# Seam into the third matrix product: conversion in shorter bursts, column pairs of 384/448/448, weights loaded step by step, more output buffers

## The chip, the cores and the metric

One core of one Trainium2 chip runs the whole program. The metric is the time of one execution on the device in microseconds (us), as the median of several runs. Smaller is better.

## The reference, cut to what matters

Inputs are `q`, `k`, `v` of shape (8, 8, 576, 64) in float32, and four weight matrices that arrive as 64-bit floats; the output is float32.

```python
q_s = softmax(q, axis=-1);  k_s = softmax(k, axis=2)          # with +1e-9 under the sums
attn = einsum('bhsd,bhde->bhse', q_s, einsum('bhsd,bhse->bhde', k_s, v))
x = attn.transpose(0, 2, 1, 3).reshape(4608, 512)
h = x @ moe_w_in                       # 512 -> 2048
g = h * (1 / (1 + exp(-1.702 * h)))
x = g @ moe_w_out                      # 2048 -> 512
h = x @ moe2_w_in                      # 512 -> 2048
g = where(h >= 1, h, where(h <= -1, 0, (h + 1) ** 2 / 4))
out = g @ moe2_w_out                   # 2048 -> 512
```

So there is one attention without a score matrix and then four matrix products over 4608 tokens.

## The kernel before, in words

Every matrix product is done on pairs (high, low) of float32r numbers: each product of a weight and an operand is three matrix multiplications (high·high, high·low, low·high). All but the first part of the first product use a seven-product scheme (Strassen-Winograd): weights and operands are split into quadrants, seven sums of quadrants are multiplied, and sums of the results give the output.

The stretches of the program, in order:

1. **Attention with the first product for four blocks.** Tokens come in nine blocks of 512. Blocks 0, 1, 2 and 4 (`CL`) are multiplied directly in 64 steps of 12 matrix multiplications (`gemm1`, L1038 to L1040). The attention of all nine blocks is laid between these steps; the table `AT` gives the step at which each block's attention starts. Results of the five other blocks go to DRAM (`xs_dram`).
2. **The pair stretch**: the first product for the remaining five blocks, 2560 tokens, with the seven-product scheme (`gemm_b`, L1358). It has 3 pairs × 4 groups × 7 products = 84 steps of 12 matrix multiplications. `PAIRS` says how many columns a step has. Behind each step, `post_b` lets ScalarE copy a bank of PSUM or VectorE add one (L209, "a sum" below); ScalarE then applies the activation (L1394) and SyncE stores the result to `g0_dram` (L1397). The stored tiles take turns in the buffers of the list `EB`.
3. **Pass 2**: the second product (`gemm2`, L1509), 5 token blocks × 7 products × 4 = 140 steps of 12. Its operands are tiles of `g0_dram`, loaded by `load_g` (L1488), split by ScalarE (high, L1190) and VectorE (low, L209) into the buffers of the list `RING`. Its weights are seven tiles of 2 MB (`load_weight`, L344), one per product.
4. **Two more passes** of 140 steps each, for the third and the fourth product (L605, L487).

The class `Weights` converts the 64-bit weights of the second, third and fourth product, each in 8 pieces while an earlier stretch runs: per piece two raw loads (L240), the conversion (L178 on ScalarE, L184 and L191 on VectorE), seven sums of quadrants and their high and low parts (L282, L209, L292), and seven stores to `wp_dram` (L304). The pieces of the second product's weights ("out1") are made during the pair stretch; pass 2 loads them from there.

A planner (`Plan.order`) puts all of this in one order per engine: each entry has an engine, an estimated duration, a rank (measured in steps), what it reads and writes, and a bonus in rank (`haste`). Engines then execute their own queue strictly in that order, SyncE too: a transfer that must wait for a buffer holds back all transfers behind it in SyncE's queue. `LAST` is 64, the rank of the first step of the pair stretch, and `NEXT` is 148, the rank of the first step of pass 2.

The lines by which the second product's weights and first operands are asked for:

```python
w_new.everything([LAST + 2 + 8 * i for i in range(8)], later)
...
for x, (tag_i, p) in zip((-13, -12, -6, -4.9, -3.9, -2.9, 0), enumerate(ORDER)):
    load_w2(w_out1, "out1", p, tag_i, NEXT + x)
for i in range(4):
    load_g(0, "11", i, NEXT - 11 + i / 4)
    load_g(0, "22", i, NEXT - (5.9, 5.8, 4.8, 4.7)[i])
    load_g(0, "12", i, NEXT - (3.8, 3.7, 2.8, 2.7)[i])
```

Of the kernel before, what the change touches and what calls it, by code (L numbers as in the profile page):

```python
# [98 lines left out]
def kernel(  # L99
# [112 lines left out]
    class Weights:  # L212
        W = 128

        def __init__(self, w, at):
            self.w, self.at, self.n, self.kept = w, at, 0, None
            self.src = {"out1": w1_out, "in2": w2_in, "out2": w2_out}[w]
            self.raw_n, self.f_n = ((w, "r", 0), (w, "r", 1)), tuple((w, "f", i) for i in range(4))
            self.h_n = ((w, "h", 0), (w, "h", 1)) + self.raw_n
# [1112 lines left out]
    def load_x(jj, qd):  # L1332
        j, c = cut(jj, int(qd[1]) - 1)
        t = x_t[jj, qd] = slot(QB[qd])[:, :, :PAIRS[jj][0]]
        nc.sync.dma_start(out=t, in_=xs_dram[j, int(qd[0]) - 1][:, :, c])
# [353 lines left out]
```

## Time and profile before

| what | value |
|---|---|
| runs | 1587.96 us median of 3 (1583.99 to 1588.44) |
| the profiled execution | 1590.3 us; its span, first to last instruction, 1588.3 us |
| TensorE busy | 1493.2 us, 94% of the span |
| VectorE busy | 1126.9 us, 71% |
| ScalarE busy | 894.5 us, 56% |
| TensorE's granted clock, mean | 0.977 of full speed |
| pair stretch | starts at 267.3 us |
| pass 2 | first multiplication at 494.5 us, last one ends at 888.8 us |

How to read it: the span is what the trace shows; the execution's own time has 2.0 us more around it. TensorE is the busiest engine, so time is lost where it stands idle or runs at a lower clock. In the views below PE is TensorE's matrix multiplications, PEld its weight loads, DVE is VectorE, ACT is ScalarE, SP is SyncE and SPq its queue of transfers.

### The profile page before, as it was taken

To read this page: it belongs to the slowest core of one execution; us is meant where nothing else is said; L and a number is where in the kernel's file an instruction comes from. 1 tells how busy PE (TensorE), PEld (TensorE's weight loads), DVE (VectorE), ACT (ScalarE), POOL (GpSimd) and SP (SyncE) were. 2 spreads that over 40 slices of the span, in tenths; PEclk is the share of its full clock that TensorE was granted. 3 is DMA by queue.
4 is the path that set the end of the run, shared out by engine and by line. 5 is a ranking of instruction groups with operands and counts; after the bars stand their busy time and mean duration, and the time that the engine had idled before them with its cause. 6 is when DMAs were issued, how large, how long until landed. Compare 5 with 4: busy or idle time off the path is not lost. (4 is left out here: it accounts for less than half of the span.)

```text
span 1588.3 us, 21360 instructions
## 1 busy us (share of the span) xinstructions
PE 1493.2 (94%) x7920; PEld 1285.5 (81%) x7920; DVE 1126.9 (71%) x1410; ACT 894.5 (56%) x1132; POOL 6.2 (0%) x27
## 2 busy tenths in 40 slices
PE   5999999999944799999999999999999999999998
PEld 3878777888843578778899888888999888888998
DVE  7999953564522679697976657585775788795885
ACT  5877774565621354545444468787786544443443
POOL 0000000000000000000000000000000000000000
PEclk9999999999986899999999999999999999999999
DMA  9978753676787375847477755564658981534441
GB/s 286 275 210 243 217 191 152 237 265 252 247 328 314 108 269 154 274 148 257 146 226 274 280 202 218 213 218 183 239 194 294 420 292 48 157 134 133 134 120 40
DMA packets 257656, 341.16 MB, mean 215 GB/s; under 512 B 93840, under 2 KB 214672, under 8 KB 254864
## 3 DMA queue, kind: packets, MB, share of 16 engines
q1 hardware_dynamic: 256752, 339.70, 62.8%
q8 instruction: 62, 1.02, 0.3%
q14 instruction: 42, 0.34, 0.1%
q10 hardware_dynamic: 800, 0.10, 0.0%
HBM read 196.08 MB, written 143.65 MB: 214 GB/s over the span
## 5 line engine op out<-in xcount | busy, mean ns | idle before, releaser
L209 DVE TENSOR_TENSOR s<-s,s 128x1024 fp32r<-128x1024 f32 (+6 forms) x692 | 608.4, 919 | 237.9 <-ACT s L1190 68.6
L1509 PE MATMUL z<-s,w 128*128 128x512 f32 (+1 forms) x1440 | 311.5, 376 | 64.2 <-ACT s L1190 50.0
L1509 PEld LDWEIGHTS z<-s,w 128*128 128x128 f32 x1440 | 267.0, 192 | 105.7 <-ACT s L1190 50.9
L1190 ACT ACTIVATE s<-s 128x1024 fp32r<-128x1024 f32 (+2 forms) x168 | 161.3, 968 | 152.3 <-PE z L1509 92.1
L455 ACT ACTIVATE s<-s 128x1024 fp32r<-128x1024 f32 (+1 forms) x140 | 136.2, 976 | 174.2 <-PE zx L487 62.1
L487 PE MATMUL z<-s,w 128*128 128x512 f32 (+1 forms) x1008 | 210.6, 368 | 0.3 <-DVE s L209 0.3
L605 PE MATMUL z<-s,w 128*128 128x512 f32 (+1 forms) x960 | 208.6, 369 | 2.4 <-ACT s L1190 2.4
L487 PEld LDWEIGHTS z<-s,w 128*128 128x128 f32 x1008 | 183.7, 188 | 25.0 <-DVE s L209 0.7
L605 PEld LDWEIGHTS z<-s,w 128*128 128x128 f32 x960 | 176.0, 189 | 25.6 <-ACT s L1190 2.8
L605 PE MATMUL zx<-s,w 128*128 128x512 f32 (+1 forms) x720 | 157.7, 367 | 0.4 <-issue 0.4
L605 PEld LDWEIGHTS zx<-s,w 128*128 128x128 f32 x720 | 131.3, 188 | 17.6 <-issue 0.8
L487 PE MATMUL zx<-s,w 128*128 128x512 f32 (+1 forms) x648 | 135.1, 367 | 0.0
L487 PEld LDWEIGHTS zx<-s,w 128*128 128x128 f32 x648 | 117.9, 188 | 15.0
L1358 PE MATMUL z<-s,w 128*128 128x512 f32 (+1 forms) x576 | 116.1, 354 | 0.7 <-ACT s L1394 0.7
L1358 PEld LDWEIGHTS z<-s,w 128*128 128x128 f32 x576 | 96.4, 190 | 16.2 <-ACT s L1394 0.9
L1038 PE MATMUL hps<-s,w 128*128 128x512 f32 x256 | 104.4, 408 | 0.0
L1040 PE MATMUL hps<-s,w 128*128 128x512 f32 x256 | 100.3, 392 | 0.0
L1039 PE MATMUL hps<-s,w 128*128 128x512 f32 x256 | 100.1, 391 | 0.0
L1358 PE MATMUL zx<-s,w 128*128 128x512 f32 (+1 forms) x432 | 88.3, 354 | 2.4 <-ACT s L1190 1.6
L1358 PEld LDWEIGHTS zx<-s,w 128*128 128x128 f32 x432 | 72.1, 189 | 14.1 <-ACT s L1190 1.8
L209 DVE TENSOR_TENSOR s<-s,z 128x1024 f32<-128x1024 f32 (+2 forms) x58 | 63.7, 1099 | 25.1 <-PE z L1358 8.6
L655 ACT ACTIVATE s<-s 128x1024 f32<-128x1024 f32 (+1 forms) x80 | 77.6, 969 | 1.0
(102 smaller groups left out, 1445.5 us busy)
## 6 DMA issues: line engine op xcount, KB each, us to landing
g<-s SPq DMA_DIRECT2D x112, 512.0 KB, 3.1
s<-g SPq DMA_DIRECT2D x96, 512.0 KB, 5.6
wp_out<-s SPq DMA_DIRECT2D x112, 256.0 KB, 2.9
w<-wp_out SPq DMA_DIRECT2D x14, 2048.0 KB, 15.1
s<-g SPq DMA_DIRECT2D x48, 384.0 KB, 4.2
s<-in_moe_w_out_dram SPq DMA_DIRECT2D x32, 512.0 KB, 4.3
wp_in<-s SPq DMA_DIRECT2D x56, 256.0 KB, 4.2
w<-wp_in SPq DMA_DIRECT2D x7, 2048.0 KB, 10.2
```

The source lines that it names most:

```text
L209: return nc.vector.tensor_tensor(out=o, in0=x, in1=y, op=op)
L455: first_of[s] = nc.scalar.activation(out=hi, in_=src, func=ACTF.Copy)
L487: nc.tensor.matmul(out=z[:, m, :n], lhsT=a, rhs=b[:, c, :], start=(at is not None and i == 0 and c == 0 and x == 0), stop=(i == 3 and c == ...
L605: nc.tensor.matmul(out=z[:, m, :n], lhsT=a, rhs=b[:, c, :], start=(p in OPENS and c == 0 and x == 0), stop=(c == 1 and x == 2), skip_group ...
L655: nc.scalar.activation(out=got["t"], in_=got["t"], func=ACTF.Square)
L1038: nc.tensor.matmul(out=hps, lhsT=wh, rhs=ah, start=(kk == 0), stop=False)
L1039: nc.tensor.matmul(out=hps, lhsT=wh, rhs=al, start=False, stop=False)
L1040: nc.tensor.matmul(out=hps, lhsT=wl, rhs=ah, start=False, stop=(kk == KD - 1))
L1190: nc.scalar.activation(out=o, in_=x, func=ACTF.Copy)
L1358: nc.tensor.matmul(out=zb[jj, g, a][:, m, :n], lhsT=w[:, f], rhs=y[:, c, :], start=(p in OPENS and c == 0 and x == 0), stop=(c == 1 and x ...
L1509: nc.tensor.matmul(out=zs2[j, a][:, m, :n], lhsT=y, rhs=b[:, c, :], start=(first and c == 0 and x == 0), stop=(i == 3 and c == 1 and x == ...
```

## The change

Six things change together.

- **Pieces of a conversion** (all three weight matrices): two raw buffers in place of one, so that both raw loads of a piece are asked for at once; the entries of one piece lie within 4.5 steps in place of 7.3. For "out1" the pieces start 5.3 steps apart from rank 58.9 in place of 8 steps apart from rank 66, and have a bonus of 1 in rank in place of a malus of 3.
- **Columns of the pairs**: 384, 448, 448 in place of 512, 512, 256. The pairs now cut across the blocks, so that a tile is loaded or stored in up to two transfers.
- **Attention** of the last seven blocks starts 6.0 steps apart (from 8.6) in place of 6.55 (from 7.5).
- **Weights of pass 2**: two of the seven are asked for before pass 2 starts (at NEXT − 16.9 and − 13.9), the other five at NEXT + 0.5, 4, 8, 12 and 16. Tiles of `g0_dram` for the first block are asked for earlier.
- **Output buffers** of the pair stretch: 4 in the first pair, 5 in the second, 8 in the third, in place of 4 throughout.
- **Operand buffers of pass 2**: the first two steps take theirs from `RING` too, whose order is changed.

```diff
-            self.raw_n, self.f_n = ((w, "r", 0), (w, "r", 1)), tuple((w, "f", i) for i in range(4))
-            self.h_n = ((w, "h", 0), (w, "h", 1)) + self.raw_n
+            self.f_n, self.h_n = (tuple((w, x, i) for i in range(4)) for x in "fh")
+            self.raw_n = self.h_n[:2], self.h_n[2:]
...
-                self.kept = a, h(b) + (c[:, :512], c[:, 512:768]), h(d) + h(a)
+                self.kept = (a, d), h(b) + (c[:, :512], c[:, 512:768]), h(a) + h(d)
...
-            w, n, x = self.w, self.W, self.n % 4
+            w, n, x = self.w, self.W, (0, 1, 2, 3, 0, 1, 2)[self.n % 7]
...
-                    self.load(si, h, later(s0 + 2 * h))
-                    self.convert(h, later(s0 + 2 * h + 1.5))
+                    self.load(si, h, later(s0 + 0.1 * h))
+                    self.convert(h, later(s0 + 1.3 + 0.5 * h))
                 for part in range(4):
-                    self.sums(si, part, later(s0 + 4.5 + 0.8 * part))
+                    self.sums(si, part, later(s0 + 2.3 + 0.6 * part))
...
-    AT.update({j: (7.5 + 6.55 * (j - 2), 10.8 + 6.55 * (j - 2)) for j in range(2, NB)})
+    AT.update({j: (8.6 + 6.0 * (j - 2), 8.6 + 3.3 + 6.0 * (j - 2)) for j in range(2, NB)})
...
-    PAIRS = ((TB, (3, 5)), (TB, (6, 7)), (TB // 2, (8, 8)))
+    REST = [j for j in range(NB) if j not in CL]
+    PAIRS = ((384, 0), (448, 768), (448, 1664))
...
-    EB = (24, 25, 26, 18)
+    E1, E2 = (24, 25, 26, 18), (19, 20, 21, 22)
+    EB = E1 * 4 + (24, 25, 26, 18, 19) * 4
+    EB = EB[:32] + (E1 + E2) * 2
...
     def cut(jj, t):
-        n, blocks = PAIRS[jj]
-        return blocks[t], slice(t * n, t * n + n) if blocks[0] == blocks[1] else slice(0, n)
+        n, t0 = PAIRS[jj]
+        return [(off, m, REST[x], slice(c, c + m)) for off, m, x, c in segs(t0 + t * n, n, TB)]
...
+            def kept():
+                for off, m, j, c in parts:
+                    nc.sync.dma_start(out=g0_dram[j][a * 4 + g][:, :, c], in_=got[0][:, :, off:off + m])
...
-    hand(LAST + 0.9, sl(*WB), w_new.names)
-    w_new.everything([LAST + 2 + 8 * i for i in range(8)], later)
+    hand(AT[NB - 1][1] + 10.88, sl(*WB), w_new.names)
+    w_new.everything([AT[NB - 1][1] + 11 + 5.3 * i for i in range(8)], lambda k: later(k, 1, 1))
     NEXT = LAST + len(steps)
-    hand(NEXT - 15, w_new.names, sl(*WB))
+    hand(LAST + 46, w_new.names, sl(*WB))
...
-                operand_b(0, x, LAST - 3 + 0.9 * i)
+                operand_b(0, x, AT[NB - 1][1] + 10.9 + 0.9 * i)
...
-    RING = (16, 17, 18, 19, 24, 25, 26)
+    RING = (16, 17, 24, 25, 26, 18, 19)
...
     def at_ring(s):
-        return (20 + 2 * s, 21 + 2 * s) if s < 2 else tuple(RING[(2 * s - 4 + x) % len(RING)] for x in range(2))
+        return tuple(RING[(2 * s + x) % len(RING)] for x in range(2))
...
-    for x, (tag_i, p) in zip((-13, -12, -6, -4.9, -3.9, -2.9, 0), enumerate(ORDER)):
+    for x, (tag_i, p) in zip((-16.9, -13.9, 0.5, 4, 8, 12, 16), enumerate(ORDER)):
         load_w2(w_out1, "out1", p, tag_i, NEXT + x)
     for i in range(4):
-        load_g(0, "11", i, NEXT - 11 + i / 4)
-        load_g(0, "22", i, NEXT - (5.9, 5.8, 4.8, 4.7)[i])
-        load_g(0, "12", i, NEXT - (3.8, 3.7, 2.8, 2.7)[i])
+        load_g(0, "11", i, LAST + 47 + i)
+        load_g(0, "22", i, NEXT - (6.9, 6.8, 5.9, 5.8)[i])
+        load_g(0, "12", i, NEXT - (4.9, 4.8, 3.9, 3.8)[i])
```

What the planner makes of it is seen at three places. The first is TensorE's queue at the seam, before: rows of L1358 are the pair stretch, rows of L1509 pass 2; a number behind a name tells tiles apart, and `s20` is buffer 20.

```order
L1509 MATMUL z_4506<-s20_4498,w_4363 128x512 x2
L1509 MATMUL z_4506<-s21_4499,w_4363 128x512
L1509 MATMUL z_4506<-s20_4498,w_4363 128x512
L1358 MATMUL z_4425<-s8_4017,w_322 128x256
L1358 MATMUL z_4425<-s9_4018,w_322 128x256
L1358 MATMUL z_4425<-s8_4017,w_322 128x256 x2
```

The first step of pass 2 stands ahead of the last three steps of the pair stretch. In the changed kernel the same place of TensorE's queue (L1367 is the pair stretch there, L1519 pass 2) reads:

```order
L1367 MATMUL zx_4480<-s10_4088,w_322 128x448 x2
L1367 MATMUL zx_4480<-s11_4089,w_322 128x448
L1367 MATMUL zx_4480<-s10_4088,w_322 128x448
L1519 MATMUL z_4581<-s16_4557,w_4312 128x512
L1519 MATMUL z_4581<-s17_4558,w_4312 128x512
```

All 84 steps of the pair stretch now stand ahead of pass 2, and no other step is mixed in.

The second place is SyncE's queue of transfers at the seam, before: `w` from `wp_out1` are weights of pass 2, `s` from `g0` its operands, `g0` from `s` the stores of the pair stretch.

```order
L1488 DMA s5_4423<-g0_1_1_99 128x1024
L344 DMA w_4452<-wp_out1_6_71 128x4096
L344 DMA w_4454<-wp_out1_5_73 128x4096
L1488 DMA s2_4456<-g0_1_6_104 128x1024
L1488 DMA s3_4470<-g0_1_7_105 128x1024
L1488 DMA s6_4472<-g0_1_2_100 128x1024
L1488 DMA s7_4474<-g0_1_3_101 128x1024
L344 DMA w_4476<-wp_out1_2_72 128x4096
L344 DMA w_4478<-wp_out1_7_70 128x4096
L1397 DMA g0_8_2_156<-s26_4341 256x1x256
L1488 DMA s12_4485<-g0_0_0_90 128x1024
```

In the changed kernel SyncE's queue reads as follows from the first weights that are asked for after the start of pass 2 (L1498 is `load_g` there, L1408 the stores, L301 the stores of the third product's converted weights).

```order
L1408 DMA g0_8_7_161<-s20_4518 256x1x64
L1408 DMA g0_8_3_157<-s22_4598 256x1x448
L344 DMA w_4707<-wp_out1_5_73 128x4096
L301 DMA wp_in2_1_76<-s8_4660 256x2x128
L301 DMA wp_in2_4_81<-s11_4663 256x2x128
L344 DMA w_4792<-wp_out1_2_72 128x4096
L301 DMA wp_in2_5_80<-s8_4660 256x2x128
L1498 DMA s4_4816<-g0_0_4_94 128x1024
L301 DMA wp_in2_2_79<-s8_4660 256x2x128
```

The weights no longer stand among the operand loads and stores of the seam, but the fifth and the later ones stand behind stores of the third product's conversion.

The third place is VectorE's queue in the changed kernel, from the last but one sum of the pair stretch on (rows that read `zx` or `z` with 448 columns); the 128x1024 rows are pass 2's: sums of quadrants in place, and low halves, which go to another buffer than they read from.

```order
L209 TENSOR_TENSOR s19_4500<-s19_4500,zx_4480 128x2x448
L209 TENSOR_TENSOR s4_4516<-s0_4478,s4_4516 128x1024
L209 TENSOR_TENSOR s17_4558<-s12_4289,s16_4557 128x1024
L209 TENSOR_TENSOR s20_4518<-s20_4518,z_4465 128x2x448
L209 TENSOR_TENSOR s5_4520<-s1_4482,s5_4520 128x1024
L209 TENSOR_TENSOR s6_4538<-s2_4498,s6_4538 128x1024
L209 TENSOR_TENSOR s25_4578<-s13_4291,s24_4577 128x1024
L209 TENSOR_TENSOR s7_4542<-s3_4502,s7_4542 128x1024
L209 TENSOR_TENSOR s12_4289<-s4_4516,s12_4289 128x1024
L209 TENSOR_TENSOR s13_4291<-s5_4520,s13_4291 128x1024
L209 TENSOR_TENSOR s24_4604<-s4_4516,s17_4603 128x1024
```

No row of the conversion of "out1" stands here any more; in the kernel before, its last row stood two rows ahead of pass 2's first. The low halves that go to buffers 17, 25 and 24 feed TensorE's first three steps of pass 2.

## Rows read from the trace of the kernel before

**Rows 1.** Busy time by stretch: busy us (instructions) of each engine, PEclk, DMA share, GB/s.

```profile
core 0 of [0], span 1588.3 us
core 0: us, PE busy (x) PEld busy (x) DVE busy (x) ACT busy (x) POOL busy (x), PEclk, DMA share, GB/s
60.00:180.00 120.00, 120.00 (x1019) 94.96 (x1018) 116.27 (x172) 92.20 (x106) 3.08 (x10) 1.00 0.78 225
180.00:267.30 87.30, 87.30 (x612) 68.81 (x611) 44.86 (x61) 52.13 (x62) 0.00 (x0) 1.00 0.54 187
267.30:458.85 191.55, 189.28 (x974) 162.37 (x972) 107.89 (x184) 115.34 (x172) 0.00 (x0) 1.00 0.69 247
458.85:494.50 35.65, 0.00 (x0) 0.00 (x0) 4.92 (x5) 2.25 (x3) 0.00 (x0) 0.56 1.02 422
494.50:560.00 65.50, 48.77 (x201) 39.07 (x202) 34.71 (x41) 24.44 (x32) 0.00 (x0) 0.82 0.46 160
560.00:888.76 328.76, 314.60 (x1517) 276.57 (x1517) 263.13 (x321) 154.41 (x202) 0.00 (x0) 0.99 0.68 224
```

**Rows 2.** TensorE's waits, whole execution: us in total, times, longest us.

```profile
PE z L1509 <- ACT s L1190: 50.0, 3, 35.7
PE z L1509 <- DVE s L209: 14.2, 12, 3.3
```

**Rows 3.** Instructions in order of time at the seam: start, us, engine, line; idle before it.

```profile
457.25 1.60 PE L1358 MATMUL z<-s,w 128*128 128x256 f32 x12
...
460.36 1.00 SPq L344 DMA_DIRECT2D w<-wp_out  x2
...
481.82 11.55 SPq L1397 DMA_DIRECT2D g<-s  x4
492.23 0.60 ACT L1394 ACTIVATE s<-z 128x512 f32<-128x512 f32 x1 [27.91 <-DMA g<-s]
493.39 1.06 ACT L1190 ACTIVATE s<-s 128x1024 fp32r<-128x1024 f32 x1 [0.56 <-DMA s<-g]
494.48 4.75 DVE L209 TENSOR_TENSOR s<-s,s 128x1024 fp32r<-128x1024 f32 x4 [11.41 <-ACT s L1190]
494.50 0.80 PE L1509 MATMUL z<-s,w 128*128 128x512 f32 x1 [35.65 <-ACT s L1190]
...
525.29 0.80 PE L1509 MATMUL z<-s,w 128*128 128x512 f32 x1 [13.49 <-ACT s L1190]
```

**Rows 4.** Two steps, 24 matrix multiplications, of 256 columns, in order of time.

```profile
443.36 3.04 PE L1358 MATMUL zx<-s,w 128*128 128x256 f32 x24
```

**Rows 5.** The chain that ended last: steps of 384 (first) and 512 columns.

```profile
843.10 2.08 PE zx L1509 x12
...
898.33 2.72 PE zx L605 x12
```

**Rows 6.** VectorE groups in 260 to 560 us by shape: busy us, mean ns, idle before.

```profile
L209 DVE TENSOR_TENSOR s<-s,s 128x256 fp32r<-128x256 f32 x54 | 22.1, 422 | 18.3 <-ACT s L282 17.8
...
L191 DVE SCALAR_TENSOR_TENSOR s<-s,s 128x512 uint32<-128x512 uint32 x18 | 12.4, 691 | 5.7 <-ACT s L178 5.5
...
L184 DVE TENSOR_SCALAR s<-s 128x512 uint32<-128x512 uint32 x18 | 7.7, 425 | 36.2 <-DMA s<-in_moe_w_out_dram 36.2
```

**Rows 7.** VectorE's sums from PSUM in the pair stretch, 512 and 256 columns.

```profile
L209 DVE TENSOR_TENSOR s<-s,zx 128x1024 f32<-128x1024 f32 x8 | 9.8, 1221 | 9.3 <-PE zx L1358 9.3
...
L209 DVE TENSOR_TENSOR s<-s,zx 128x512 f32<-128x512 f32 x4 | 2.8, 688 | 6.3 <-PE zx L1358 6.2
```

**Rows 8.** Transfers, whole execution: count, KB each, median us from issue to landing.

```profile
s<-g SPq DMA_DIRECT2D x96, 512.0 KB, 5.6
wp_out<-s SPq DMA_DIRECT2D x112, 256.0 KB, 2.9
w<-wp_out SPq DMA_DIRECT2D x14, 2048.0 KB, 15.1
...
s<-in_moe_w_out_dram SPq DMA_DIRECT2D x32, 512.0 KB, 4.3
```

**Rows 9.** SyncE's waits, 260 to 560 us: us in total, times, longest us.

```profile
SPq L344 <- PE zx L1358: 13.4, 2, 13.2
```

More of the change, by code (lines that the diff above doesn't have):

```diff
@@ L230, in load @@
             n = self.W
-            raw = lambda: self.area()[0].bitcast(I64)
+            raw = lambda: self.area()[0][i].bitcast(I64)
             if self.w == "in2":
@@ L243, in load @@
                 )
-            put(0, "SP", 560, fn, (), self.raw_n, moves=10.5 * n)
+            put(0, "SP", 560, fn, (), self.raw_n[i], moves=10.5 * n)
         def convert(self, i, put):
@@ L1328, in cut, with load_x, fn @@
     def cut(jj, t):
-        n, blocks = PAIRS[jj]
-        return blocks[t], slice(t * n, t * n + n) if blocks[0] == blocks[1] else slice(0, n)
[L1332 to L1335, printed above, removed]
+        n, t0 = PAIRS[jj]
+        return [(off, m, REST[x], slice(c, c + m)) for off, m, x, c in segs(t0 + t * n, n, TB)]
+    def load_x(jj, qd, rank, after):
+        n, h, parts = PAIRS[jj][0], int(qd[0]) - 1, cut(jj, int(qd[1]) - 1)
+        def fn():
+            t = x_t[jj, qd] = slot(QB[qd])[:, :, :n]
+            for off, m, j, c in parts:
+                nc.sync.dma_start(out=t[:, :, off:off + m], in_=xs_dram[j, h][:, :, c])
+        add("SP", 560 * len(parts), rank, fn, after + tuple(("xs", j, h) for _, _, j, _ in parts), sl(QB[qd]),
+            moves=2.5 * n)
     def operand_b(jj, p, r, haste=0):
@@ L1388, in finish @@
         def finish(make, e, src, src_n, a, t, haste=0):
-            j, c = cut(jj, t)
-            got = []
+            parts, got = cut(jj, t), []
             def gelu():
@@ L1396, in finish @@
             add("ACT", act, s + 1.2, gelu, src_n, e, haste=haste, table="gelu")
-            add("SP", 420, s + 1.3, lambda: nc.sync.dma_start(out=g0_dram[j][a * 4 + g][:, :, c], in_=got[0]), e,
-                (("g0", j),), moves=2.5 * n)
+            def kept():
+                for off, m, j, c in parts:
+                    nc.sync.dma_start(out=g0_dram[j][a * 4 + g][:, :, c], in_=got[0][:, :, off:off + m])
+            add("SP", 420 * len(parts), s + 1.3, kept, e, tuple(("g0", x[2]) for x in parts), moves=2.5 * n)
         def more(name, a, t):
@@ L1426, in post_b, with later @@
             finish(make, e, z, z_n, 0, int(p == 3), -4 * (p == 3))
-    def later(k0, lag=1):
+    def later(k0, lag=1, haste=-3):
         def put(k, engine, ns, fn, reads, writes, moves=0):
-            add(engine, ns, k0 + k, fn, reads + step(int(k0 + k) - lag), writes, moves, haste=-3)
+            add(engine, ns, k0 + k, fn, reads + step(int(k0 + k) - lag), writes, moves, haste=haste)
         return put
@@ L1445 @@
             for qd in ("11", "12", "22", "21"):
-                add("SP", 560, LAST - 14, lambda qd=qd: load_x(0, qd), step(LAST - 15), sl(QB[qd]), moves=1270)
+                load_x(0, qd, LAST - 14, step(LAST - 15))
             for i, x in enumerate(PROD):
-                operand_b(0, x, LAST - 3 + 0.9 * i)
+                operand_b(0, x, AT[NB - 1][1] + 10.9 + 0.9 * i)
         tag = ({1: W_TAG[g // 2], 2: W_TAG[g // 2], 4: W_TAG[2 + g // 2], 3: W_TAG[2 + g // 2]} | T_TAG)[p]
@@ L1455 @@
                 for qd in ("11", "12", "22", "21"):
-                    add("SP", 560, s, lambda jj=jj, qd=qd: load_x(jj + 1, qd),
-                        step(s - 1) + (("xs", cut(jj + 1, int(qd[1]) - 1)[0], int(qd[0]) - 1),),
-                        sl(QB[qd]), moves=2.5 * PAIRS[jj + 1][0])
+                    load_x(jj + 1, qd, s, step(s - 1))
             if g == 3:
```

12 lines of the change are left out of this document (6 added, 6 removed).

## The prediction

> **What bounds the kernel now.** I read the stretches first. TensorE is the engine to watch: from 60 to 267 us it is never idle, from 267.30 to 458.85 us it is busy for 189.28 of 191.55 us, then for 35.65 us it does nothing, then until 560 us it is busy for 48.77 of 65.50 us at a granted clock of 0.82, and to the end of pass 2 it is busy for 314.60 of 328.76 us [rows 1]. Of the waits, the three of pass 2 on ScalarE cost 50.0 us and the twelve on VectorE 14.2 us [rows 2].
>
> How much is lost in each stretch shows against the work in it. A step of 12 matrix multiplications takes 2.72 us at 512 columns and 2.08 at 384 [rows 5]: 0.005 us per column. So 448 columns take 2.40 and 256 take 1.44, which the trace bears out (3.04 for two steps less 1.60 for one) [rows 3, 4]. The pair stretch is 28 × (2.72 + 2.72 + 1.44) = 192.6 us of work, pass 2 is 84 × 2.72 + 56 × 2.08 = 345.0 us. From 267.30 to 888.76 us are 621.5 us, so 83.9 us are lost:
>
> - until 458.85 us: 81 steps, 56 × 2.72 + 25 × 1.44 = 188.3 us of work in 191.55: 3.2 us lost;
> - 458.85 to 560 us: 3 steps of 1.44 and 1680 − 1517 = 163 multiplications of pass 2 at 2.72 / 12, together 41.3 us, in 101.15 us: 59.9 us lost, idle time and lowered clock in one (0.56 in the gap, 0.82 behind it);
> - 560 to 888.76 us: 308.0 us of work in 328.76: 20.7 us lost.
>
> Why there is a gap shows in the order of time [rows 3]. The first step of pass 2 stands in TensorE's queue ahead of three steps of the pair stretch, and its operand is late. ScalarE, which must make it (493.39), stood for 27.91 us before an activation whose output buffer was still being stored; the stores stood in SyncE's queue behind loads of weights and operands and took 11.55 us to issue at 481.82, and the transfers ran flat out, at 422 GB/s with a share of 1.02 [rows 1]. The second gap of 13.49 us, at 525.29, is the same knot: one weight load waits 13.2 us in SyncE's queue for TensorE to leave its buffer [rows 9], with stores behind it.
>
> **The change part by part.**
>
> *Columns.* 28 × (2.08 + 2.40 + 2.40) = 192.6 us: the same work. VectorE's and ScalarE's instructions stay as many over the same columns. The pairs cut across blocks, so there are 40 more transfers (8 loads, 32 stores), spread over some 190 us in a queue that mostly waits; nothing, as SyncE has no other work. If they came all at the seam, at 0.5 us per issue (1.00 us for two at 460.36 [rows 3]), they would cost 20 us there.
>
> *Earlier conversion, and bursts.* All 8 pieces already lie in the pair stretch, where VectorE is busy for 107.89 of 191.55 us [rows 1]. One piece costs VectorE 2 × 0.425 + 2 × 0.691 + 11 × 0.422 = 6.9 us [rows 6], eight cost 55 us. In the new order the last piece ends in the first group of the third pair, so the same 108 us less some 6 of sums fall into about 62 steps, 56 × 2.24 + 6 × 2.40 = 140 us, and a lead of five steps: about two thirds. A sum that is late stalls TensorE, because product 3 writes the bank that product 5's sum reads, one step later. Lower bound nothing; upper bound: each piece's wait for raw data (36.2 us in 12 waits, 3.0 each [rows 6]) plus a sum of 1.1 us, less the step of 2.2 us, 8 times, 15 us. VectorE has a third of its time free there, so I take 5 us in place of 3.2: **+1.8 us**. What it buys is that the weights are in DRAM some 20 steps before pass 2.
>
> *Attention 6.0 steps apart.* VectorE is busy for 116.27 of 120 us up to 180 us, but only for 44.86 of the 87.30 after it [rows 1]. The change takes 3.3 steps, at 2.72 us and the attention's share some 12 us, from the distance; 42 us are free behind. Between nothing and 12 us, I take nothing, since TensorE waits nowhere there now.
>
> *Weights and operands at the seam.* Five loads of 2 MB leave the seam, 10.5 MB, which at 422 GB/s [rows 1] are 25 us of transfers, and the stores no longer stand behind them; with 8 buffers in the last pair, ScalarE's activation has a buffer from the pair's previous turn. TensorE's queue has no foreign step ahead of the pair stretch's end. So the knot goes, **−59.9 us**, and what takes its place is VectorE's queue. I walk it from pass 2's first multiplication as time 0. The sum behind product 5 can start at −2 × 2.40 = −4.8 us and takes 1.1 (between 1.22 at 512 and 0.69 at 256 columns [rows 7]); an operation on a pass 2 tile takes 4.75 / 4 = 1.19 us [rows 3]. By the order shown: a sum and the first low half, done at −1.3 (in time); the last sum of the pair stretch, two sums, the second low half, done at 3.3, wanted at 2.7; four operations on, done at 8.1, wanted at 6.0. From there a step costs VectorE about 2.4 of 2.72 us. That is **+2.6 us**. For the rest of the first block I take the rate of the later ones, 20.7 us over 1517 / 12 = 126 steps, for 28 steps: **+4.6 us**. Lower bound of the two: nothing, if everything lands early; upper bound: the rivals below.
>
> Do transfers allow it? The first block's 28 steps, 76 us, carry five weight loads (10.5 MB), 16 operand tiles (8.4 MB), about 2.3 pieces of the third product's conversion at 2 × 512 and 7 × 256 KB (6.7 MB) and 4 stores (2.1 MB) [sizes in rows 8]: 27.7 MB, 363 GB/s. The gap moved 422 GB/s [rows 1], so the transfers are at 86%: no term. The Trainium skill, "DMA: Bandwidth & Descriptors", section "Specifications", puts the limit of memory at about 358 GB/s per core; by that the block would need 77.4 us, 1.2 us more than TensorE's work. The trace disagrees: 422 GB/s over 35.65 us. The sum goes by the trace.
>
> *Pass 2 behind it* keeps its 20.7 us (VectorE 263.13 of 328.76 us busy, by the waits on L209), the passes after it theirs: zero either way.
>
> Sum: 1588.3 − 59.9 + 1.8 + 2.6 + 4.6 = 1537.4 us of span, 1539.4 of its own time (2.0 us around the span). The profiled execution, 1590.3, lies 2.3 us above the median, so **1537 us**.
>
> **The rivals.**
>
> *A. Weights late in pass 2.* In the new order the fifth weights (product 2) stand behind two stores of the third product's conversion, whose data VectorE makes 21 large and some 9 small operations after the first low half: at about 27 us. The load lands 15.1 us later [rows 8], at 42; they are wanted 16 steps on, at 43.5 + 2.6. With transfers at 86% a load may take twice as long: 11 us late, and product 3 and 4 behind it some more: 1537 + 11 to 20, about 1553. For it: one load already waits 13.2 us in that queue [rows 9]. Against: 4 us to spare by the medians. The Trainium skill, same page, section "Anatomy of one DMA — SWDGE (gpsimd) path", says that a wait is served on the issuing sequencer, not by the transfer engines; by that rule everything behind the stores waits too, which is this rival, and the trace agrees.
>
> *B. Conversion ahead of sums in the pair stretch*: the upper bound above, 15 in place of 5 us, and late operands with it: about 1551. For it: the pieces now come with a bonus. Against: two raw loads at once halve the waits.
>
> *C. More than the seam.* The bursts leave VectorE free between them, and the 20.7 us of pass 2 go by half: 1527; with the pair stretch free too, 1522. For it: fewer waits for raw data. Against: the sums of pass 2 are as many.
>
> *D. Slower: the knot is tied elsewhere.* The third weights' load stands ahead of the stores of buffers 18 and 19, from which pass 2's third and fourth operands are made; if it waits for its buffer until TensorE needs those, there is again a gap of 35.65 and one of 13.49 us at half the clock, 59.9 together: 1588.3 + 1.8 + 4.6 = 1594.7 of span, about 1594. It decides only from 51 us of new loss. Against: its buffer is free 5 steps before pass 2.
>
> *E. The conversion is late as before* and the burst of loads just moves into pass 2: within 5 us of before.
>
> **How the numbers follow.** The forecast has 0.61, C 0.14, A 0.10, B 0.08, E 0.03, D 0.04. The forecast alone reaches from 1529 to 1547. To leave out no more than 2 in 10 the range takes C's lower time, some below it, and A's upper end: 1518 to 1557. Within 0.3% is about 5 us, what a measurement can tell from no change. Faster 0.93, same 0.03, slower 0.04.
>
> **What would show it.** Right: no idle time of TensorE over 5 us between 420 us and the end of pass 2; the clock at 1.00 across the seam; pass 2 starting near 465 us and ending near 838 us; first waits of pass 2 on L209. Wrong: a wait on a weight load or of ScalarE on a store at the seam (D, E), idle time in the pair stretch over 8 us (B), stalls some 16 to 24 steps into pass 2 (A), or TensorE waiting before 260 us, where I took nothing.

## The result, and the profile after

The changed kernel takes **1544.6 us** (median of 4 runs, 1543.8 to 1545.5) beside 1587.8 us of the kernel before on the same chip: ratio 0.9733, 95% interval 0.9716 to 0.975. The prediction was 1537 us, 1518 to 1557. The profiled execution took 1543.8 us, its span 1541.8.

The stretches, columns as in [rows 1]; the pair stretch now ends and pass 2 begins at 473.09, pass 2 ends at 843.31:

```profile
60.00:263.90 203.90, 203.90 (x1614) 160.87 (x1614) 163.64 (x238) 155.70 (x179) 3.08 (x10) 1.00 0.70 211
263.90:473.09 209.19, 201.24 (x1022) 187.56 (x1022) 107.15 (x182) 118.87 (x177) 0.00 (x0) 0.99 0.78 264
473.09:560.00 86.91, 79.24 (x338) 62.35 (x337) 68.69 (x80) 40.34 (x52) 0.00 (x0) 1.00 0.90 333
560.00:843.31 283.31, 273.39 (x1346) 243.44 (x1345) 229.82 (x282) 135.18 (x177) 0.00 (x0) 0.99 0.66 219
310.00:315.00 5.00, 3.19 (x10) 3.19 (x11) 2.67 (x8) 4.07 (x8) 0.00 (x0) 0.66 0.59 203
```

The stretch without TensorE, 35.65 us in [rows 1], has no counterpart. TensorE's waits, as in [rows 2] (L1519 is pass 2's line, L1367 the pair stretch's, L1190 a copy or high half on ScalarE, L209 a sum or low half on VectorE):

```profile
PE z L1519 <- DVE s L209: 16.0, 16, 1.8
...
PE z L1367 <- ACT s L1190: 3.7, 2, 2.6
...
PE zx L1367 <- ACT zx L1190: 2.2, 2, 1.2
PE zx L1519 <- ACT zx L1190: 1.2, 1, 1.2
PE z L1367 <- ACT s L1044: 1.1, 1, 1.1
PE zx L1367 <- ACT s L1190: 0.9, 2, 0.5
```

The wait of pass 2 on ScalarE, 50.0 us before, is down to 1.5 us (1.2 and 0.3); that on VectorE is 16.0 us instead of 14.2. The pair stretch waited 3.1 us in all before; now it waits 7.9 us on ScalarE (3.7 + 2.2 + 1.1 + 0.9). And the seam in order of time, as in [rows 3]:

```profile
470.65 2.60 PE L1367 MATMUL zx<-s,w 128*128 128x448 f32 x12
473.09 3.12 PE L1519 MATMUL z<-s,w 128*128 128x512 f32 x13
477.82 3.01 PE L1519 MATMUL z<-s,w 128*128 128x512 f32 x12 [1.61 <-DVE s L209]
482.37 5.75 PE L1519 MATMUL z<-s,w 128*128 128x512 f32 x24 [1.53 <-DVE s L209]
489.28 5.51 PE L1519 MATMUL z<-s,w 128*128 128x512 f32 x23 [1.16 <-DVE s L209]
495.95 3.02 PE L1519 MATMUL zx<-s,w 128*128 128x512 f32 x12 [1.16 <-ACT zx L1190]
498.80 5.60 PE L1519 MATMUL z<-s,w 128*128 128x512 f32 x24
```

No foreign step stands among those of the pair stretch, the last step runs into pass 2 without idle time, and the first waits are on L209, as the prediction asked. Pass 2 starts at 473 and ends at 843 us, where it said 465 and 838.

Measured with the prediction's own accounts (the work is 2.72 us of stage 1 still to come at 263.90, 192.6 of the pair stretch and 345.0 of pass 2):

| place | predicted us lost | measured | from |
|---|---|---|---|
| pair stretch | 5.0 | 13.8 | 209.19 − 2.72 − 192.64 |
| first block of pass 2, to 560 | 2.6 + 4.6 = 7.2 | 10.3 | 86.91 − 338 × 2.72 / 12 |
| pass 2 behind it | 20.7 | 14.9 | 370.22 − 345.0 − 10.3 |
| stage 1 | 0 | −0.7 | 263.90 + 2.72 against 267.30 |
| behind pass 2 | 0 | −1.0 | 1541.8 − 843.31 against 1588.3 − 888.76 |

The deviations, 8.8 + 3.1 − 5.8 − 0.7 − 1.0, are the 4.4 us by which the span is over the forecast of 1537.4. The other 3 us: I took 2.3 us off because the profiled execution of before lay above its median; here it lies 0.8 below.

### The profile page after: what moved, and what is told of

It is laid out like the page before. It is cut to its first block, busy times and chain, and to the rows that moved or that the text cites. A ratio compares the mean times of both kernels' runs of the same rounds, so it can differ in the third digit from the quotient of the medians.

```text
span 1541.8 us, 21375 instructions
## 1 busy us (share of the span) xinstructions
PE 1490.0 (97%) x7920; PEld 1297.4 (84%) x7920; DVE 1125.3 (73%) x1410; ACT 904.2 (59%) x1140; POOL 6.2 (0%) x27
## 4 chain that ended last, share of the span: by engine, by line
PE 77%; DMA 12%; DVE 6%; ACT 2%; issue 2%; SPq 1%; DVEq 0%; ACTq 0%
PE z L605 13%; PE z L487 12%; PE z L1519 10%; PE zx L605 9%; PE zx L487 9%; DVE s L209 5%; PE hps L1038 4%; PE z L1367 4%; PE hps L1040 4%; PE hps L1039 4%; DMA g<-s 3%; PE zx L1367 3%; DMA s<-g 3%; PE zx L1519 3%; DMA wp_in<-s 2%
## 5 line engine op out<-in xcount | busy, mean ns | idle before, releaser
L209 DVE TENSOR_TENSOR s<-s,s 128x1024 fp32r<-128x1024 f32 (+7 forms) x692 | 607.6, 918 | 190.4 <-ACT s L282 40.4
L1519 PE MATMUL z<-s,w 128*128 128x512 f32 (+1 forms) x1440 | 305.3, 370 | 16.4 <-DVE s L209 16.0
L1519 PEld LDWEIGHTS z<-s,w 128*128 128x128 f32 x1440 | 262.3, 189 | 57.3 <-DVE s L209 23.0
L1190 ACT ACTIVATE s<-s 128x1024 fp32r<-128x1024 f32 (+2 forms) x168 | 161.3, 969 | 151.5 <-PE z L1519 89.5
L487 PE MATMUL z<-s,w 128*128 128x512 f32 (+1 forms) x1008 | 210.6, 368 | 0.5 <-DVE s L209 0.5
L605 PE MATMUL z<-s,w 128*128 128x512 f32 (+1 forms) x960 | 207.2, 367 | 2.4 <-ACT s L1190 2.4
L487 PEld LDWEIGHTS z<-s,w 128*128 128x128 f32 x1008 | 183.8, 188 | 25.2 <-DVE s L209 0.9
L605 PEld LDWEIGHTS z<-s,w 128*128 128x128 f32 x960 | 175.0, 188 | 25.2 <-ACT s L1190 2.8
L605 PE MATMUL zx<-s,w 128*128 128x512 f32 (+1 forms) x720 | 157.7, 367 | 0.4 <-issue 0.4
L605 PEld LDWEIGHTS zx<-s,w 128*128 128x128 f32 x720 | 131.3, 188 | 17.6 <-issue 0.8
L487 PE MATMUL zx<-s,w 128*128 128x512 f32 (+1 forms) x648 | 135.1, 367 | 0.0
L487 PEld LDWEIGHTS zx<-s,w 128*128 128x128 f32 x648 | 117.9, 188 | 14.9
L1367 PE MATMUL z<-s,w 128*128 128x448 f32 (+1 forms) x576 | 118.6, 359 | 4.8 <-ACT s L1190 3.7
L1367 PEld LDWEIGHTS z<-s,w 128*128 128x128 f32 x576 | 106.8, 190 | 11.8 <-ACT s L1190 4.4
L1367 PE MATMUL zx<-s,w 128*128 128x448 f32 (+1 forms) x432 | 89.2, 357 | 3.2 <-ACT zx L1190 2.2
L282 ACT ACTIVATE s<-s 128x256 fp32r<-128x256 f32 x168 | 64.7, 410 | 38.6 <-DMA wp_in<-s 18.3
L209 DVE TENSOR_TENSOR s<-s,z 128x1024 f32<-128x1024 f32 (+2 forms) x58 | 63.6, 1097 | 32.0 <-PE z L1367 7.4
L1367 PEld LDWEIGHTS zx<-s,w 128*128 128x128 f32 x432 | 78.8, 188 | 9.4 <-ACT zx L1190 3.0
```

Of the source, the lines that this page charges most:

```text
L209: return nc.vector.tensor_tensor(out=o, in0=x, in1=y, op=op)
L282: nc.scalar.activation(out=hi, in_=src, func=ACTF.Copy, scale=-1.0 if neg else 1.0)
L487: nc.tensor.matmul(out=z[:, m, :n], lhsT=a, rhs=b[:, c, :], start=(at is not None and i == 0 and c == 0 and x == 0), stop=(i == 3 and c == ...
L605: nc.tensor.matmul(out=z[:, m, :n], lhsT=a, rhs=b[:, c, :], start=(p in OPENS and c == 0 and x == 0), stop=(c == 1 and x == 2), skip_group ...
L1190: nc.scalar.activation(out=o, in_=x, func=ACTF.Copy)
L1367: nc.tensor.matmul(out=zb[jj, g, a][:, m, :n], lhsT=w[:, f], rhs=y[:, c, :], start=(p in OPENS and c == 0 and x == 0), stop=(c == 1 and x ...
```

## The experiments

Each is the changed kernel with one edit, unless it says otherwise. "Pair" and "pass 2" are the us lost there in the profiled execution, worked out as in the table above (13.8 and 25.2 in the changed kernel).

| run | median us | ratio, 95% interval | pair | pass 2 |
|---|---|---|---|---|
| e1 old weight times | 1567.1 | 0.987 (0.9851 to 0.989) | 15.9 | 49.4 |
| e2 four buffers | 1570.7 | 0.9889 (0.9867 to 0.9912) | 30.1 | 37.9 |
| e3 pairs 512/512/256 | 1547.0 | 0.9736 (0.9712 to 0.976) | 12.6 | 30.8 |
| e4 handicap for the conversion | 1549.9 | 0.9757 (0.9737 to 0.9778) | 13.5 | 30.4 |
| e5 pairs 448/448/384 | 1541.9 | 0.972 (0.9704 to 0.9735) | 11.6 | 28.1 |
| e6 conversion later than its load | 1553.7 | 0.979 (0.9776 to 0.9805) | 12.8 | 25.1 |
| e7 e5 and e6 | 1552.8 | 0.9788 (0.9771 to 0.9804) | 9.2 | 29.5 |
| e8 before, new weight times | 1571.2 | 0.9898 (0.9882 to 0.9915) | | |
| e9 third product's conversion later | 1555.6 | 0.9806 (0.9784 to 0.9827) | 16.8 | 31.0 |
| e10 conversion and sums later, pair stretch alone | 1546.8 | 0.9745 (0.9719 to 0.977) | 14.4 | 24.9 |
| e11 conversion starts 2 steps later | 1554.1 | 0.98 (0.9779 to 0.982) | 22.7 | 26.4 |
| e12 old attention spacing | 1543.6 | 0.9722 (0.9703 to 0.9741) | 10.7 | 27.9 |

The runs of e3, e10 and e12 spread over 6 to 9 us, so differences under some 4 us tell nothing here.

The column "pair" has a scatter of its own. In e9 and e10 the instructions of every engine up to pass 2 come in the same order as in the changed kernel, by line, tile name and shape, and they show 16.8 and 14.4 beside 13.8. The column also counts from 263.90 us in every run, where stage 1 has 11 to 21 multiplications left (12 in the changed kernel); in e4, with 21, that makes 2.0 of the 13.5 us. So differences under some 3 us in it tell nothing either.

**Which part took the gap away: e1, e2, e8.**

```
-    for x, (tag_i, p) in zip((-16.9, -13.9, 0.5, 4, 8, 12, 16), enumerate(ORDER)):
+    for x, (tag_i, p) in zip((-13, -12, -6, -4.9, -3.9, -2.9, 0), enumerate(ORDER)):
```

> The changed kernel with the old times of the weight loads of pass 2 (all seven asked for around the seam). If the gap of before came from these loads standing ahead of stores and operands in SyncE's queue, a gap of TensorE comes back at the seam, some 14 to 36 us, and the time is 1558 to 1580 us. Rival: the earlier conversion and the further output buffers untie the knot by themselves; then TensorE is nowhere idle over 5 us at the seam and the time stays within 5 us of 1545 us.

Measured 1567.1 us, 22.5 above the changed kernel: the rival falls. The trace of this kernel from 475 to 520 us (by stretch), then SyncE's and ScalarE's instructions in order of time (L1408 stores an output):

```profile
475.00:520.00 45.00, 18.47 (x67) 14.11 (x66) 17.78 (x16) 8.22 (x8) 0.00 (x0) 0.70 0.80 315
```

```profile
482.81 17.30 SPq L1408 DMA_DIRECT2D g<-s  x6
...
509.86 1.06 ACT L1190 ACTIVATE s<-s 128x1024 fp32r<-128x1024 f32 x1 [23.59 <-DMA g<-s]
```

It is the old knot: six stores take 17.30 us to issue behind the loads, ScalarE's high half stands 23.59 us for a buffer that a store still reads, TensorE is busy for 18.47 of 45 us, and the granted clock is 0.70.

```
-    EB = EB[:32] + (E1 + E2) * 2
+    EB = E1 * 12
```

> The changed kernel with four output buffers in all pairs. If ScalarE's activation at the seam waits for a store again, pass 2 starts late: the trace shows the line of the activation waiting on a DMA, and the time is 1550 to 1560 us. Rival: with the loads gone from the queue the stores go out in time, four buffers do, and the time stays within 5 us of 1545 us.

Measured 1570.7 us, 26.1 above, more than either theory gave. The loss begins inside the pair stretch already, 30.1 us against 13.8, with waits of 3.00, 5.55 and 1.18 us in its last 20 us:

```profile
468.95 19.32 SPq L1408 DMA_DIRECT2D g<-s  x6
...
479.81 0.92 ACT L1190 ACTIVATE s<-zx 128x896 f32<-128x896 f32 x1 [8.78 <-DMA g<-s]
```

Here it is not the activation (L1402) that waits longest for a store, but the copy out of the bank (L1190), 8.78 us, and TensorE waits 5.6 us for that copy.

```
(in the kernel before)
-    for x, (tag_i, p) in zip((-13, -12, -6, -4.9, -3.9, -2.9, 0), enumerate(ORDER)):
+    for x, (tag_i, p) in zip((-16.9, -13.9, 0.5, 4, 8, 12, 16), enumerate(ORDER)):
```

> The kernel before with only the new times of the weight loads of pass 2. Theory (weights as needed work only with a conversion that is done early and with output buffers for the last pair): the gap stays for the greater part, the time is 1570 to 1590 us. Rival (the loads' place in the queue is all): 1548 to 1555 us.

Measured 1571.2 us: 16 of the 43 us, as the theory had it. ScalarE still stands 20.7 us for output stores and TensorE 35.6 us for ScalarE at the seam. So loads and buffers each are worth 22 to 26 us when one alone is taken back, and the loads 16 when they are put in alone: the gap has two causes in one queue, and went only where both went. Whether the conversion must be early too, and what the earlier operand tiles and the new order of `RING` are worth, was not tried by itself and stays open.

**What the pair stretch loses: e3, e4, e5.** My theory after reading the trace was this. In the changed kernel, ScalarE and then TensorE in order of time (L178 is the conversion of raw weights):

```profile
305.20 0.68 ACT L178 ACTIVATE s<-s 128x512 f32<-128x512 f32 x1 [2.39 <-DMA s<-in_moe_w_out_dram]
...
308.56 0.66 ACT L178 ACTIVATE s<-s 128x512 f32<-128x512 f32 x1 [1.98 <-DMA s<-in_moe_w_out_dram]
...
310.96 0.79 ACT L1190 ACTIVATE s<-z 128x768 f32<-128x768 f32 x1
```

```profile
311.81 5.86 PE L1367 MATMUL z<-s,w 128*128 128x384 f32 x24 [2.55 <-ACT s L1190]
```

ScalarE stands twice for raw data, the copy that frees a bank stands behind, TensorE waits 2.55 us, and its clock is at 0.66 from 310 to 315 us. With steps of 2.08 us there is little slack for that.

```
-    PAIRS = ((384, 0), (448, 768), (448, 1664))
+    PAIRS = ((512, 0), (512, 1024), (256, 2048))
```

> The changed kernel with pairs of 512, 512 and 256 columns. The pair stretch loses 13.8 us in the changed kernel, most of it in the first pair, whose step of 384 columns is 2.08 us. Theory (conversion ahead of the copies that free PSUM banks, felt most where the step is short): the first pair loses less, some 4 us in place of 8, but the last pair of 1.44 us a step meets what is left of the conversion and the start of pass 2, so the time is 1545 to 1560 us with the loss in the last pair. Rival (the narrow first pair alone is the cause): the loss of the pair stretch goes by 6 us or more with no new one, 1536 to 1540 us.

Measured 1547.0 us, and the loss moved as the theory said: TensorE's idle time from 263.9 to 340 us falls from 6.3 us to 1.8 (36.10 − 34.55 and 40.00 − 39.77), and two waits, 4.2 us together, come up shortly before pass 2, in the steps of 1.44 us. The first of them:

```profile
465.45 2.93 PE L1367 MATMUL zx<-s,w 128*128 128x256 f32 x12 [3.46 <-ACT s L1190]
```

```
-    ... lambda k: later(k, 1, 1))
+    ... lambda k: later(k, 1, -1))
```

> The changed kernel with the conversion pieces of the pair stretch given a handicap of 1 step where the changed kernel gives a bonus of 1. Theory (ScalarE's queue holds conversions that wait for raw data, 2.4 us each, ahead of the copies that free banks): ScalarE's waits on the raw data there fall from 13.9 us and TensorE's waits on ScalarE in the first pair with them; the pair stretch loses 7 to 9 us in place of 13.8, the time is 1538 to 1541 us. Rival (crowding at the start of the stretch by the attention's end and the first operands, whatever the bonus): no change, within 2 us of 1545 us.

Measured 1549.9 us, and the theory falls in this form: ScalarE's waits for raw data are 16.2 us instead of 13.9, and the pair stretch loses 13.5 (11.5 without what stage 1 has left over). The time is 5 us longer, lost in pass 2 (30.4). One of the two stalls behind raw data goes, the other comes again at 295.89 us with 2.21.

```
-    PAIRS = ((384, 0), (448, 768), (448, 1664))
+    PAIRS = ((448, 0), (448, 896), (384, 1792))
```

> The changed kernel with pairs of 448, 448 and 384 columns: the short step of 2.08 us moves from the first pair to the last. Theory (a step of 2.08 us is too short for ScalarE's copies in the first pair): TensorE's idle time from 263.9 to 340 us falls from 6.3 us to about 2, as with 512 columns (1.8), the last pair loses 1 to 2 at the seam, and the time is 1539 to 1542 us. Rival (what the short steps lose they lose wherever they stand, as 256 columns did in the last pair): 1544 to 1549 us.

Measured 1541.9 us. Idle time from 263.9 to 340 us is 3.3 us (36.10 − 32.84, and none behind), half of the changed kernel's. The pair stretch gains 2.2 us and pass 2 gives 2.9 back; the interval overlaps that of the changed kernel, so the runs do not separate the two.

Where pass 2 gives it back shows in e5's rows, TensorE, VectorE and SyncE:

```profile
476.19 0.50 PE L1519 MATMUL z<-s,w 128*128 128x512 f32 x1 [2.43 <-ACT s L1190]
482.41 16.48 PE L1519 MATMUL z<-s,w 128*128 128x512 f32 x59 [5.72 <-DVE s L209]
```

```profile
481.13 3.62 DVE L209 TENSOR_TENSOR s<-s,s 128x1024 fp32r<-128x1024 f32 x3 [3.75 <-DMA g<-s]
```

```profile
467.76 9.97 SPq L1408 DMA_DIRECT2D g<-s  x6
```

It is the old knot in small: six stores take 9.97 us to issue, VectorE stands 3.75 us for a store, and the first seven steps of pass 2 lose 13.0 us where the changed kernel loses 6.7. In e3, e4 and e7 a wait of 4.2 to 5.8 us stands at the same place, and the first seven steps lose 9.5, 11.8 and 13.1 us.

**Raw data: e6, e7, e10.** One step between load and conversion, and for the sums:

```
-                    self.convert(h, later(s0 + 1.3 + 0.5 * h))
+                    self.convert(h, later(s0 + 2.3 + 0.5 * h))
-                    self.sums(si, part, later(s0 + 2.3 + 0.6 * part))
+                    self.sums(si, part, later(s0 + 3.3 + 0.6 * part))
```

> The changed kernel with the conversion of every piece of the pair stretch one step later than its raw load, and its sums too. Theory (ScalarE stands before a conversion whose raw data is still on the way, and copies that free banks stand behind it): ScalarE's waits on the raw data fall from 13.9 to under 7 us, TensorE's waits on ScalarE in the first pair from 7.9 to 3 to 5 us, and the time is 1540 to 1542 us. Rival (the waits hide nothing that TensorE needs; the copies are late by themselves): the waits on the raw data go and the time stays within 2 us of 1545 us.

> Both: pairs of 448, 448 and 384 columns, and the conversion one step later than its load. If the two losses are separate, the gains add up, 1535 to 1540 us. Rival: they are the same waits, and the time is that of the better of the two.

In both, the raw data of a piece is loaded before the last halves of the piece ahead are written to the same buffers, so that part of the weights comes from other data; the work is the same. The edit was wider than I meant: the two later conversions go through the same lines, and a later pass (L487) gets its first weights late. TensorE's waits behind pass 2 in e6:

```profile
PE z L487 <- DMA w<-wp_out: 5.5, 1, 5.5
```

So the times, 1553.7 and 1552.8 us, say nothing of the pair stretch; its own account does. ScalarE's waits for raw data sink from 13.9 to 8.4 us (2.5 before L178, 5.9 before L282), the stalls at 293.78 and 311.81 us go, but others come (2.04 us at 326.17), and the stretch loses 12.8 instead of 13.8. TensorE's waits on ScalarE in it fall from 7.9 to 6.2 us, not to the 3 to 5 of the theory. With 448 columns first it loses 9.2, the least of all, and the start of pass 2 gives it back (29.5 after 25.2).

```
-        def everything(self, starts, later):
+        def everything(self, starts, later, lead=0):
(convert and sums at s0 + lead + ..., lead 0.7 in the pair stretch)
```

> The changed kernel with conversion and sums 0.7 of a step later behind their raw loads, in the pair stretch alone (the earlier run with one step moved the two later conversions too). Theory (waits of ScalarE for raw data ahead of the copies that free banks): TensorE's idle time from 263.9 to 340 us falls from 6.3 to about 3 us, the time is 1540 to 1542 us. Rival (the copies are late by their own chain, bank to ScalarE to bank): the waits on raw data shrink, TensorE's idle time there stays at 5 to 7 us, the time within 2 us of 1545 us.

Measured 1546.8 us, the pair stretch 14.4. But ScalarE's waits for raw data stayed at 13.8 us: 0.7 of a step did not take the conversion out from ahead of the copies, so this run does not try the theory. By line, tile name and shape the instructions of every engine stand in the changed kernel's order from the first to the last, so it is in effect a second measurement of the changed kernel.

**Place of the pieces: e11, e12.**

```
-    w_new.everything([AT[NB - 1][1] + 11 + 5.3 * i ...
+    w_new.everything([AT[NB - 1][1] + 13 + 5.3 * i ...
```

> The changed kernel with all eight pieces of the pair stretch's conversion two steps later. Theory (crowding where the attention ends and the first conversion and the first operands meet): TensorE's idle time from 263.9 to 300 us falls from 3.75 to under 2 us, the time is 1541 to 1543 us. Rival (the place of the pieces does not matter, the short steps do): idle time there as before, within 2 us of 1545 us, or up to 3 us more since the last piece ends nearer to pass 2.

Measured 1554.1 us, 9.5 more, which neither gave: the pair stretch loses 22.7. The same mechanism, larger. ScalarE in order of time, and what TensorE waited:

```profile
289.80 0.69 ACT L178 ACTIVATE s<-s 128x512 f32<-128x512 f32 x1 [2.64 <-DMA s<-in_moe_w_out_dram]
293.20 0.67 ACT L178 ACTIVATE s<-s 128x512 f32<-128x512 f32 x1 [2.72 <-DMA s<-in_moe_w_out_dram]
...
295.41 0.79 ACT L1190 ACTIVATE s<-z 128x768 f32<-128x768 f32 x1
...
350.45 0.92 ACT L1190 ACTIVATE s<-z 128x896 f32<-128x896 f32 x1 [3.34 <-DMA g<-s]
```

```profile
296.25 6.02 PE L1367 MATMUL z<-s,w 128*128 128x384 f32 x24 [3.69 <-ACT s L1190]
...
351.42 6.74 PE L1367 MATMUL z<-s,w 128*128 128x448 f32 x24 [4.32 <-ACT s L1190]
```

The first is the wait for raw data, 3.69 us on TensorE. The second is another: the copy waits 3.34 us for an output buffer that a store still reads. Of the 8.9 us that the stretch loses more, 5.2 are idle time (13.2 instead of 8.0), and most of the rest is that steps of 448 columns take 2.48 us here instead of 2.43 (last section).

```
-    AT.update({j: (8.6 + 6.0 * (j - 2), 8.6 + 3.3 + 6.0 * (j - 2)) for j in range(2, NB)})
+    AT.update({j: (7.5 + 6.55 * (j - 2), 10.8 + 6.55 * (j - 2)) for j in range(2, NB)})
```

> The changed kernel with the attention blocks 6.55 steps apart again instead of 6.0, which also puts the conversion of the pair stretch, hung on the last block's place, 2.2 steps later. Theory (the closer attention is worth something only because the conversion can start earlier; two steps later cost 9 us in the run before this): the stretch to 263.9 us is as long as in the changed kernel within 1 us, the pair stretch loses 20 to 24 us in place of 13.8, the time is 1551 to 1557 us. Rival (the spacing is worth nothing, as the prediction took it): within 2 us of 1545 us.

The theory falls, the rival holds: 1543.6 us, although the conversion starts 2.2 steps later here as well. The difference to e11 is that the attention's end and the first operands move with it. ScalarE's waits for raw data come to 14.7 us in e12's pair stretch and 9.1 in e11's, TensorE's idle time there to 4.7 and 13.2 us. So neither how late the pieces come nor how long ScalarE stands for raw data sets the cost; the rows above suggest that it is what stands behind those waits in ScalarE's queue, which no run moved by itself.

**Start of pass 2: e9.**

```
-    w_new2.everything([NEXT + 3 + 12 * i for i in range(8)], later)
+    w_new2.everything([NEXT + 19 + 12 * i for i in range(8)], later)
```

> The changed kernel with the conversion of the third product's weights, which lies in pass 2, started 16 steps later (43 us). Theory (the 10.3 us lost in the first block of pass 2 are VectorE's: the sums and low halves of the conversion on top of the operands'): the loss of that block falls to the walked 3 to 5 us, what is taken out comes back later with a few us at most, and the time is 1539 to 1542 us. Rival (the operands and sums alone keep VectorE behind, or what is saved is lost again when the conversion comes): within 2 us of 1545 us.

The first block by stretch:

```profile
476.02:560.00 83.98, 76.19 (x325) 61.03 (x324) 60.23 (x60) 36.14 (x40) 0.00 (x0) 0.99 0.80 299
```

83.98 − 325 × 2.72 / 12 = 10.3 us lost, the same sum as with the conversion in it, but not at the same place. The first seven steps lose 6.8 us here and 6.7 in the changed kernel. Behind them, in the changed kernel:

```profile
498.80:517.80 19.00, 19.00 (x85) 15.76 (x84) 12.07 (x20) 7.59 (x12) 0.00 (x0) 1.00 0.70 227
517.80:560.00 42.20, 40.00 (x170) 31.12 (x170) 35.33 (x42) 21.86 (x29) 0.00 (x0) 1.00 1.03 388
```

and in e9, whose first conversion (L178) runs at 542.80 us:

```profile
501.82:542.80 40.98, 40.98 (x182) 33.97 (x181) 25.63 (x22) 17.66 (x17) 0.00 (x0) 1.00 0.68 247
542.80:563.43 20.63, 18.36 (x73) 14.33 (x72) 16.37 (x25) 10.23 (x16) 0.00 (x0) 0.92 0.93 325
```

Behind the first seven steps TensorE is never idle as long as the conversion is out; once it has begun, the loss comes back. So the loss at the start of pass 2 is not the conversion's, and the 3.6 us behind it come with the conversion. In the changed kernel (first L178 at 496.76 us) ScalarE shows how:

```profile
516.46 0.42 ACT L282 ACTIVATE s<-s 128x256 fp32r<-128x256 f32 x1 [5.74 <-DMA wp_in<-s]
```

A row of the conversion waits 5.74 us for a store of converted weights, operands stand behind it, and TensorE's next wait is at 518.87 us. The rival's second half holds: what is saved is lost again when the conversion comes. In all the run is 11 us slower: of these, 5.8 are lost in pass 2 (one wait on L209 of 5.43 us at 720.39), and 2.9 in a pair stretch whose order is the changed kernel's. The operands' own chain, behind the loss of the first steps, stands in the trace of the changed kernel, ScalarE and VectorE:

```profile
475.79 1.06 ACT L1190 ACTIVATE s<-s 128x1024 fp32r<-128x1024 f32 x1 [1.16 <-PE z L1519]
480.42 1.06 ACT L1190 ACTIVATE s<-s 128x1024 fp32r<-128x1024 f32 x1 [3.57 <-PE z L1519]
484.98 1.07 ACT L1190 ACTIVATE s<-s 128x1024 fp32r<-128x1024 f32 x1 [3.50 <-PE z L1519]
```

```profile
476.54 9.42 DVE L209 TENSOR_TENSOR s<-s,s 128x1024 fp32r<-128x1024 f32 x8 [1.44 <-DMA g<-s]
```

VectorE stands 1.44 us for a store and then has eight operations in one run; TensorE waits for it step by step, and ScalarE's next high half waits for TensorE's step, which frees a buffer of the ring.

## Why the prediction was right, and where its terms were not

- **The seam, −59.9 us**: right, in mechanism and size. The rows show no idle time over 1.61 us at the seam and a clock of 1.00. e1, e2 and e8 show its cause: the loads in SyncE's queue and the buffers behind them. The prediction named both but priced them as one; they don't add up. Of its signs of being wrong one came in small, as ScalarE waits 2.3 us for stores between 440 and 500 us, and one was just missed, as TensorE is idle for 7.95 us in the pair stretch where over 8 was named.
- **Pair stretch, "I take 5 us in place of 3.2: +1.8 us"**: this step failed; measured 13.8. I looked for late sums on VectorE and took the smaller end because VectorE has a third of its time free. The waits are on ScalarE's copies, of which I said that they "stay as many over the same columns". What the rows account for: 8.0 us of idle time (209.19 − 201.24), of it 3.75 in the two stalls behind raw data and 2.2 in two waits at the start; 1.7 us because 448 columns take 2.43 and not 2.40 us; 1.5 us of lowered clock (the two steps from 311.81 us take 5.70 us, not 4.16). Some 2.3 us more lie beside the eight waits, 0.29 us at each: the step ahead of a wait ends 0.16 us later than the next would start (ends of multiplications are modelled in the trace), and the step behind it takes 0.13 us longer. Rows at two of them:

```profile
290.34 2.25 PE L1367 MATMUL z<-s,w 128*128 128x384 f32 x12
293.78 4.46 PE L1367 MATMUL z<-s,w 128*128 128x384 f32 x24 [1.20 <-ACT s L1190]
298.56 2.37 PE L1367 MATMUL zx<-s,w 128*128 128x384 f32 x12 [0.33 <-ACT s L1190]
300.77 2.24 PE L1367 MATMUL z<-s,w 128*128 128x384 f32 x12
```

293.78 − 1.20 − 290.34 = 2.24 us and 300.77 − 298.56 = 2.21 us, where a step of 384 columns takes 2.08.

The upper bound of 15 us held, and the rival B, "conversion ahead of sums", was nearer here than the forecast, though copies, not sums, stood behind. The stalls behind raw data are shown in rows, but e6 without them gains only 1 us, less than the scatter, since others take their place. Nor is the short first step a cause by itself: to 340 us TensorE is idle for 1.8 us in e3 and 3.3 in e5, which have wide first pairs, but also for only 2.2 us in e12, which has 384 columns first. What sets the loss, with its reach from 9.2 to 22.7 us by small moves, stays open.
- **Start of pass 2, "walked on VectorE's queue: +2.6 us"**: mis-sized. From 473.09 to 498.80 are 7 steps, 19.0 us of work in 25.7: 6.7 us. I began the walk as if buffers and operands were there; the wait on a store (1.44 us) and the ring (3.57 and 3.50 us on ScalarE) were left out. e3, e4, e5 and e7 show the same place at 9.5 to 13.1 us; in the last three VectorE stands 3.75 to 4.55 us for a store.
- **Rest of the first block, +4.6 us**, for 28 steps, so 3.5 for the 21 behind the start: measured 10.3 − 6.7 = 3.6. Right; by e9 it comes with the third product's conversion.
- **Behind it "its 20.7 us"**: 14.9. 14 steps, 2.3 us at that rate, I counted twice: the stretch from 560 us of before began 163 multiplications into pass 2. The other 3.5 us are a gain that I had given to rival C alone; TensorE has three waits over 2 us there before (2.05, 2.16 and 3.29) and none in the changed kernel, but why was not tried.
- **Attention, 0**: right, by the stretch from 60 to 263.9 us (never idle) and by e12.
- **Transfers "at 86%: no term"**: right. 333 GB/s × 86.91 us are 28.9 MB beside 27.7 estimated, and no wait of TensorE on a weight load came, so rival A did not happen; neither did D nor E.

That the span came out only 4.4 us over the forecast is in part luck: 8.8 + 3.1 = 11.9 us of loss more than forecast stand against 5.8 + 0.7 + 1.0 = 7.5 us less, and 2.3 of these are the double count.

No version is clearly faster than the changed kernel; e5 with 1541.9 us is the lowest, and its interval overlaps.

## What to carry to other kernels

When a store, a load and a buffer stand in one knot, price the parts together: the last one taken out brings all the gain, the first only part of it. In a stretch that gets new work, look at every queue that it is put into, not at the engine that carries most of it: an instruction that waits 2 us for data costs more by what stands behind it than by its own length. And where several stages follow each other, count what is won in one against what the next loses; here e5 and e7 gave back in the first steps of pass 2 what they won before it. Last, a changed time that leaves every queue's order as it was, like e10's, is a repeat: it tells nothing of the theory, but it shows how much an account by stretch scatters.

## What the runs showed of the hardware that I had not expected

A step of 12 multiplications of 448 columns takes 2.43 or 2.48 us, not the 2.40 that lies between 384 (2.08) and 512 (2.72). The level holds for tens of steps, and often changes behind a wait. In e10, with the granted clock at 1.00 before (380 to 396 us) and behind (400 to 416):

```profile
391.62 2.64 PE L1367 MATMUL zx<-s,w 128*128 128x448 f32 x12
394.10 2.64 PE L1367 MATMUL z<-s,w 128*128 128x448 f32 x12
396.95 2.70 PE L1367 MATMUL zx<-s,w 128*128 128x448 f32 x12 [0.22 <-ACT s L1190]
399.49 2.59 PE L1367 MATMUL z<-s,w 128*128 128x448 f32 x12
401.92 2.60 PE L1367 MATMUL zx<-s,w 128*128 128x448 f32 x12
```

The starts lie 2.48 us apart ahead of the wait of 0.22 us and 2.43 behind it. Earlier in e10 the distance went from 2.43 to 2.48 where the trace shows no wait; the two steps from 354.30 us take 5.08 us there, so a short one may lie hidden. Over 56 steps the two levels differ by 2.8 us; e11 and, behind its first 300 us, e5 ran at 2.48 for nearly all their 448-column steps, which alone moves the column "pair" by as much as most edits do. Why is open; steps of 384 columns show one level, 2.08 us, where no wait is near.
